# Five-tile openings, a multiply moved to VectorE, ordered store waits and an earlier cast in a linear-attention plus swish-MLP kernel

## The chip, the cores and the metric

The kernel runs on one core of a Trainium2 chip. The metric is device time in microseconds (us) of one execution. All times below are us unless marked ns. The engines are TensorE (PE, with its weight load PEld), VectorE (DVE), ScalarE (ACT), GpSimd (POOL) and SyncE (SP), whose queue issues most DMAs.

## The reference

Eight batches of eight heads, 576 tokens, head size 64. The attention is linear: the softmax of q runs over the head size and the softmax of k over the tokens, so that a 64x64 matrix per head stands between k, v and q. Its output, 4608 tokens of 512 features, goes through a two-layer MLP of width 2048 with the activation h * sigmoid(beta * h), whose beta is one number per hidden feature.

```python
q_s = softmax(q, axis=-1); k_s = softmax(k, axis=2)
kv  = einsum('bhsd,bhse->bhde', k_s, v)
x   = einsum('bhsd,bhde->bhse', q_s, kv)      # -> [4608, 512]
h   = x @ w_in                                # [4608, 2048]
out = (h / (1 + exp(-beta * h))) @ w_out      # [4608, 512]
```

## The kernel before, in words

**Slabs.** The MLP runs over nine slabs of 512 tokens: slab t (0 to 7) holds the first 512 tokens of batch t, and slab 8 the last 64 tokens of all eight batches. While slab t goes through the MLP, the attention of batch t+1 is worked in between, so that its output XT (bf16, features by tokens) is ready when slab t+1 begins.

**Pass 1 of a slab** makes 16 tiles of hidden features. A tile is four matmuls (m = 0 to 3, one for each 128 input features, each reading XT of that m) of 512 columns into one PSUM bank. ACT reads the bank with Silu (L746) into GT, then DVE scales by 1/beta (scale_g, L769) and, on the way, adds pieces of GT up for pass 2 (L800, L805). Tiles rotate over three banks (HB = 0, 1, 2). A slab opens with pass1_lead: the first three tiles side by side, m = 0 of all three, then m = 1, and so on, so that late XT parts are wanted late. The tile after that goes into bank 3, the following ones round the three again.

**Pass 2 of a slab** (pass2_fast, slabs 1 to 8) multiplies GT with w_out as a 2x2 block product in Winograd's form: seven block products of 256-column matmuls (L846) into the bank s and the two banks OB = 3 and 4 (called z5 and z2), and sums and differences of blocks by DVE. g_diff(0) and g_diff(1) (L812, 128x2048, bf16) are two such differences, made in place in GT, and the last two products read them. ACT copies (L882) and DVE adds (L894) move the banks to O2S, which is stored at the slab's end. The last two steps are an ACT copy of z2 and, after the last product, a DVE add of z2.

**The attention in between.** exp of q and k on ACT (L319); a sum of 64 elements (L357), a reciprocal (L359) and a multiply (L361) make the softmax of q. From batch 2 on the multiply runs on POOL, for two head pairs at a time (128x1024), and then SP issues a DMA transpose from EQ to QT (turn, L606). POOL also casts v to bf16 (L377, and L391 for remainders). kv products (L482 for batches 2 and up, two groups of two head pairs), a reciprocal RC (L490) and KVD (L459) on DVE; then the quad: four products of 64x64 tiles (L554) of KVD with QT into two banks, one for each XT part, whose copies go to XT (L596, even parts on DVE, odd ones on ACT). quad(b, (0,)) makes XT parts 0 and 1 from the first two head pairs, quad(b, (1,)) parts 2 and 3 from the others.

**What sets the order.** The program is a list of operations in the order of the Python code; each engine runs its own in that order, and waits on semaphores are derived from reads and writes of named buffers and banks. A list todo of (tick, step) pairs sets the attention steps: tick counts matmuls of the slab from its first (pass 2 by 32/56 for each matmul), and the step is put at that place in all engines' queues. Besides, pass2_fast has numbered hooks 0 to 7 between its products. For batches 2 and 3 (made in slabs 1 and 2) the order is: hook 0 exps; hook 2 sums, multiply and transpose of head pairs 0 and 1; hook 3 the same for 2 and 3 and g_diff(0), then the loads of batch t+3 (SP's queue); at tick 97 or 100 the kv products and g_diff(1); tick 118 the first quad; and after the opening's first matmuls, at tick 1.5 of the next slab, the second quad. In hook 4 ACT loads the Silu table (L1054); in slab 2 batch 4's exps of q come ahead of it.

**Batch 1** is made at the end of slab 0 with the simpler products (L406 for kv, KVD by L449), pair by pair: cast of v on DVE (L377), kv products, RC, KVD, output product.

**The end.** SP waits for all store semaphores (L151) in the order of their names, and then the program ends.

The opening, as it stands:

```python
LEAD = tuple((n, m) for m in range(NM) for n in range(3))

def pass1_lead(t, fs, tick):
    bks = [HB[(hrot[0] + n) % 3] for n in range(3)]
    hrot[0] += 3
    for n, m in LEAD:
        pass1_mm(t, fs[n], m, bks[n])
        tick()
```

Of the kernel before, what the change touches and what calls it, by code (L numbers as in the profile page):

```python
# [18 lines left out]
NF = DFF // 128  # L19
NM = DM // 128  # L20
NG = NF // 2
# [23 lines left out]
class Program:  # L45
# [83 lines left out]
    def emit(self, nc, es):  # L129
        counts, waits = self.plan()  # L130
        sems = {}
        for key in counts:
            sems[key] = es.enter_context(nc.semaphore("s_" + "_".join(str(x) for x in key)))
        by = {e: [] for e in (PE, ACTE, DVE, POOL, SP)}
        for op, w in zip(self.ops, waits):
            by[op.eng].append((op, w))

        def run(eng):
            def body(h):
                for op, w in by[eng]:  # L140
                    for key, n in w:
                        h.wait_ge(sems[key], n)
                    ins = op.fn(h)
                    if op.slot is not None:
                        ins.then_inc(sems[op.count[0]], 16)
                    elif op.inc:
                        ins.then_inc(sems[op.count[0]], 1)
                if eng == SP:
                    for key, n in sorted(counts.items(), key=str):
                        if key[0] == "dma" and str(key[1]).startswith("out"):  # L150
                            h.wait_ge(sems[key], n)  # L151
            return body

        with nc.Block() as blk:
            for e in (PE, ACTE, DVE, POOL, SP):
                getattr(blk, e)(run(e))


def bass_efficient_attn_shen__then__act_swish_beta_kernel(
# [12 lines left out]
    with ExitStack() as es:  # L172
# [48 lines left out]
        HB = (0, 1, 2)  # L221
        OB = (3, 4)
        MB = (5, 6, 7)

        P = Program()
# [376 lines left out]
        def turn(b, hp0, n):  # L602
            i = b % 2
            o = bass.AP(QT[i], hp0 * 512, [[2048, 128], [128, 4 * n], [1, 128]])
            a = bass.AP(EQ[i], hp0 * 512, [[2048, 128], [1, 512 * n]])
            add(SP, lambda e: e.dma_start_transpose(o, a),  # L606
                r=[("eq", i, hp) for hp in range(hp0, hp0 + n)],
                w=[("qt", i, hp) for hp in range(hp0, hp0 + n)], slot=f"tq{i}{hp0}")
# [6 lines left out]
        def norm_turn(b, hp0):  # L615
            norm_main(b, hp0, 2, POOL)
            turn(b, hp0, 2)

        def norm_turn_rem():
            norm_rem()  # L620
            turn_rem()

        def one(fn, *a):
            return lambda: fn(*a)

        def steps(fn, *a):
            return lambda: go(fn(*a))
# [8 lines left out]
        def attn_late(b):  # L636
            if b < 4:
                x = 100 if b == 2 else 97
                return [(x, steps(kv_all, b)), (x + .1, lambda: g_diff(1)),
                        (118, one(quad, b, (0,)))]  # L640
            return [(96, steps(kv_all, b)), (99, lambda: g_diff(1)), (112, one(quad, b))]

# [95 lines left out]
        hrot = [0]  # L738
# [16 lines left out]
                pass1_mm(t, f, m, bk)  # L755
                tick()

        LEAD = tuple((n, m) for m in range(NM) for n in range(3))

        def pass1_lead(t, fs, tick):  # L760
            bks = [HB[(hrot[0] + n) % 3] for n in range(3)]
            hrot[0] += 3
            for n, m in LEAD:
                pass1_mm(t, fs[n], m, bks[n])
                tick()

# [43 lines left out]
        def g_diff(fh):  # L810
            f, th = NG * fh, 1 - fh
            add(DVE, lambda e: e.tensor_tensor(gv(f, th, NG), gv(f, th, NG), gv(f, 1 - th, NG),  # L812
                                               ALU.subtract),
                r=gk(f, 0, NG) + gk(f, 1, NG), w=gk(f, th, NG), war=True)
# [140 lines left out]
        for t in range(NSLAB):  # L955
            todo = []
            if t == 0:
                todo = [(x, steps(t_steps, 1, (hp,), NOW, ACTE))
                        for hp, x in enumerate((97, 106, 114, 119))]
                todo += [(107, one(exp_kr_s, 1))]  # L960
                todo += [(x, one(exp_k, 1, hp, 1)) for hp, x in enumerate((108, 115, 120, 125.5))]
                todo += [(x, one(cast_v, 1, hp, DVE))
                         for hp, x in ((1, 118.5), (2, 123), (3, 127))]
                todo += [(x, steps(kv_steps, 1, (hp,), NOW))
                         for hp, x in enumerate((118, 122, 126))]
                todo += [(x, steps(out_step, 1, hp, NOW, ACTE)) for hp, x in enumerate((122.5, 125))]
                todo += [(117, one(o2_evac, 0, 0, 3, ACTE))]
                todo += [(2, steps(out_step, 0, 3, HEAD, DVE))]
            elif t < 4:
                todo = attn_late(t + 1)  # L970
                if t > 1:
                    todo += [(1.5, one(quad, t, (1,)))]
                if t == 3:
                    todo += [(4, one(norm_turn, 4, 2))]
                if t == 1:
                    todo += [(1, steps(out_step, 1, 2, (3,), ACTE)),
                             (3, steps(kv_steps, 1, (3,), (7,))),
                             (6, steps(out_step, 1, 3, (7,), DVE)),
                             (6.1, one(w_sum, 2, 4, 4)), (6.2, one(w_diff, 0)),
                             (6.3, one(w_diff, 1))]  # L980
            elif t < 7:
                todo = attn(t + 1)
            elif t == 7:
                todo = spread(outr_steps(1), 32, 48)
            todo = sorted(todo, key=lambda x: -x[0])
# [7 lines left out]
            def ftile(n):  # L993
                return n if t == 0 else n // 2 + NG * (n % 2)

            for n in range(NF + 1):
                if n == 0:
                    pass1_lead(t, [ftile(x) for x in range(3)], tick)
                elif 2 < n < NF:
                    pass1_tile(t, ftile(n), tick, 3 if n == 3 else None)  # L1000
                if n:
                    scale_g(ftile(n - 1))
                    for i_, w_ in {8: ((0, 4),), 12: ((4, 2),), 14: ((6, 1),), 16: ((7, 1),)}.get(
                            n if t else 0, ()):
                        g_sum1(i_, w_)
                        g_sum2(i_, w_)
                    if t == 2 and n == 2:
                        for hp in range(NHP):
                            cast_v(3, hp, after=P.writer[("gt", 0, 0)])
                if t == 0 and n == 14:  # L1010
                    w_sum(1)
                if t == 1 and n in (4, 7, 10):
                    o2_evac(0, n // 3, 3 + n // 3, ACTE)
                    if n == 10:
                        store(0)
# [28 lines left out]
            def on(n, fn, *a):  # L1044
                hooks.setdefault(n, []).append(lambda: fn(*a))
# [8 lines left out]
                add(ACTE, lambda e: e.activation(DUMMY[:, 2:3], WARM[:, 0:1], ACT.Silu),  # L1054
                    r=["warm"], w=["dummy"])

            def casts(b):
                g = P.writer[("gs2", NG - 1)]
                if b % 2 == 0:
                    cast_vr(b, after=g)  # L1060
                for hp in range(NHP):
                    cast_v(b, hp, after=g)

            if t == 1:
                on(0, exps, 2)
                on(0, casts, 2)
                on(2, norm_turn, 2, 0)
                on(3, norm_turn, 2, 2)
                on(3, g_diff, 0)
                on(4, silu_table)  # L1070
                on(3, load, 4)
            elif t == 2:
                on(0, exps, 3)
                on(2, norm_turn, 3, 0)
                on(3, norm_turn, 3, 2)
                on(3, g_diff, 0)
                on(3, load, 5)
                on(4, exp_q, 4)
                on(4, silu_table)
                on(4, casts, 4)  # L1080
                on(6, norm_turn, 4, 0)
            elif t == 3:
                on(0, exp_k, 4)
                on(0, exp_kr, 4)
                on(0, exp_q, 5)
                on(3, g_diff, 0)
                on(4, norm_turn, 5, 0)
                on(5, norm_turn, 5, 2)
                on(4, exp_qr, 1)
                on(5, exp_k, 5)  # L1090
                on(5, norm_turn_rem)
                on(5, casts, 5)
                on(5, load, 6)
                on(7, load_rem, "qrf", qt_h, QRF, 4)
            elif t + 2 < B:
                b = t + 2
                on(0, exps, b)
                on(0, casts, b)
                if t == 4:
                    on(0, load, 7)  # L1100
                on(3, norm_turn, b, 0)
                on(4, norm_turn, b, 2)
# [40 lines left out]
```

The softmax here doesn't subtract the row's maximum and nothing guards it: scores larger than these inputs give would overflow.

## Time and profile before

| what | value |
|---|---|
| median of 8 runs | 272.8 us (272.5 to 274.31) |
| the profiled execution's own time | 272.85 us |
| its span, first to last instruction | 271.1 us |
| granted TensorE clock, mean | 0.998 |
| TensorE / VectorE / ScalarE / GpSimd busy | 97% / 71% / 67% / 23% |
| slab 1, pass 2 | about 61 to 75 us |
| slab 2, pass 1 and pass 2 | about 75 to 89 and 89 to 104 us |
| slab 3, pass 1 and pass 2 | about 104 to 118 and 118 to 132 us |

The profile is of one execution. Its span is 1.75 us shorter than that execution's time. "Busy" of TensorE counts the tail of each matmul, which overlaps the next, so that idle time is understated: two matmuls of 512 columns that follow each other at once start 0.216 apart and are shown as 0.379 long. A few matmul records are missing from the trace, among them the first of the openings. In lines of the timeline the columns are start, length, engine, line of the kernel, operation, output and input with their shapes, and the count of merged instructions; in brackets stands the idle time of the engine before it and what ended it.

### The profile page before, as it was taken

Reading aid. Unit: us, or ns where it says so; the run is one execution under the profiler, and the core shown is the slowest. Engines: PE = TensorE matmul, PEld = TensorE weight load, DVE = VectorE, ACT = ScalarE, POOL = GpSimd, SP = SyncE. Lnnn points to the kernel's source line nnn. Section 1 sums busy time; section 2 is a strip of 40 time slices with the busy share of each in tenths; the row PEclk is TensorE's granted clock in tenths of the full one; section 3 lists DMA queues with packets and bytes.
Section 4 is the critical chain, followed back from the end, with each engine's and each line's share of the span. In section 5 each row is a group of like instructions: output and inputs, shape, how many; then the busy total and the mean of one; then the engine's idle time right before and its main releaser. Section 6 shows DMA issues by size and latency. Waiting matters only on the chain.

```text
span 271.1 us, 4991 instructions
## 1 busy us (share of the span) xinstructions
PE 262.1 (97%) x1974; PEld 163.1 (60%) x1993; DVE 193.1 (71%) x407; ACT 181.3 (67%) x289; POOL 63.1 (23%) x80
## 2 busy tenths in 40 slices
PE   8899999999999999999999999999999999999994
PEld 3444444448744875468645864587458745874683
DVE  5964586887967798868778876887588448626762
ACT  4988558789467974887778937892883387018610
POOL 2890010006530089100810660036000100000000
PEclk9999999999999999999999999999999999999999
DMA  7999999999599129940489899503600130012006
GB/s 214 322 205 207 225 327 352 294 257 376 139 325 303 67 49 295 282 155 2 78 278 282 263 357 155 184 4 77 213 2 0 37 139 2 0 59 98 0 1 156
DMA packets 59368, 45.95 MB, mean 170 GB/s; under 512 B 28609, under 2 KB 58321, under 8 KB 58321
## 3 DMA queue, kind: packets, MB, share of 16 engines
q1 hardware_dynamic: 54480, 40.90, 53.3%
q0 software_dynamic: 4240, 4.19, 9.3%
q10 hardware_dynamic: 624, 0.53, 0.6%
q8 instruction: 16, 0.26, 0.4%
q14 instruction: 8, 0.06, 0.1%
HBM read 36.71 MB, written 9.44 MB: 170 GB/s over the span
## 4 chain that ended last, share of the span: by engine, by line
PE 84%; DVE 7%; DMA 2%; ACT 2%; SPq 2%; issue 1%; DVEq 0%
PE PS L406 49%; PE PS L846 33%; DMA VF<-in_v_dram 2%; DVE QS L357 2%; PE PS L482 1%; PE PS L554 1%; DVE GT L812 1%; SPq L290 1%; SPq L278 1%; ACT EQ L319 1%; DVE EQ L361 1%; DVE VB L377 1%; DVE QI L359 0%; ACT L1054 0%; ACT O2S L882 0%
## 5 line engine op out<-in xcount | busy, mean ns | idle before, releaser
L406 PE MATMUL PS<-XT,WIN 128*128 128x512 bf16 x560 | 125.3, 379 | 1.2 <-issue 0.3
L746 ACT ACTIVATE GT<-PS,BETA 128x512 bf16<-128x512 f32 x144 | 95.2, 690 | 39.5 <-PE PS L406 39.2
L406 PEld LDWEIGHTS PS<-XT,WIN 128*128 128x128 bf16 x576 | 54.9, 98 | 64.9 <-DVE XT L596 0.7
L769 DVE TENSOR_SCALAR GT<-GT,RB 128x512 bf16<-128x512 bf16 x144 | 52.8, 387 | 38.3 <-ACT GT L746 37.6
L361 POOL TENSOR_TENSOR EQ<-EQ,QI 128x1024 bf16<-128x1024 bf16 (+1 forms) x13 | 25.6, 1967 | 48.5 <-DVE QI L359 47.8
L846 PE MATMUL PS<-WSUM,GT 128*128 128x256 bf16 x256 | 30.1, 273 | 1.2 <-ACT O2S L882 1.0
L846 PE MATMUL PS<-WOUT,GS 128*128 128x256 bf16 x256 | 31.1, 273 | 0.0
L846 PE MATMUL PS<-WOUT,GT 128*128 128x256 bf16 x256 | 29.8, 273 | 0.0
L846 PEld LDWEIGHTS PS<-WSUM,GT 128*128 128x128 bf16 x256 | 24.8, 98 | 5.2 <-issue 1.3
L882 ACT COPY O2S<-PS 128x512 f32<-128x512 f32 (+1 forms) x17 | 9.4, 559 | 26.1 <-PE PS L846 26.1
L846 PEld LDWEIGHTS PS<-WOUT,GT 128*128 128x128 bf16 x256 | 24.8, 98 | 3.0
L846 PEld LDWEIGHTS PS<-WOUT,GS 128*128 128x128 bf16 x256 | 24.8, 98 | 3.0
L319 ACT ACTIVATE EQ<-QF 128x512 bf16<-128x512 f32 x32 | 17.9, 619 | 7.8 <-DMA QF<-in_q_dram 7.7
L805 DVE TENSOR_TENSOR GS<-GT 128x512 bf16<-128x512 bf16 (+2 forms) x32 | 21.9, 685 | 0.0
L812 DVE TENSOR_TENSOR GT<-GT 128x2048 bf16<-128x2048 bf16 x16 | 21.7, 1383 | 0.0
L377 POOL CAST VB<-VF 128x512 bf16<-128x512 f32 x24 | 15.6, 649 | 21.9 <-DVE GS L805 13.3
L357 DVE TENSOR_REDUCE QS<-EQ 128x16 f32<-128x1024 bf16 (+1 forms) x20 | 19.8, 988 | 0.9 <-ACT EQ L319 0.9
L319 ACT ACTIVATE EK<-KF 128x512 bf16<-128x512 f32 x32 | 18.1, 620 | 0.2
L894 DVE TENSOR_TENSOR O2S<-TS,PS 128x512 f32<-128x512 f32 (+1 forms) x17 | 10.8, 647 | 9.7 <-PE PS L846 9.7
L846 PE MATMUL PS<-WSUM,GS 128*128 128x256 bf16 x128 | 16.6, 273 | 0.0
L406 PE MATMUL PS<-WOUT,GT 128*128 128x512 bf16 x62 | 15.0, 379 | 0.1
L846 PEld LDWEIGHTS PS<-WSUM,GS 128*128 128x128 bf16 x128 | 12.5, 98 | 3.2
(90 smaller groups left out, 207.1 us busy)
## 6 DMA issues: line engine op xcount, KB each, us to landing
out_dram<-O2S SPq DMA_DIRECT2D x8, 1024.0 KB, 4.9
QF<-in_q_dram SPq DMA_DIRECT2D x6, 1024.0 KB, 6.5
KF<-in_k_dram SPq DMA_DIRECT2D x6, 1024.0 KB, 9.3
VF<-in_v_dram SPq DMA_DIRECT2D x6, 1024.0 KB, 12.4
KF<-in_k_dram SPq DMA_DIRECT2D x8, 256.0 KB, 5.6
VF<-in_v_dram SPq DMA_DIRECT2D x8, 256.0 KB, 5.6
WOUT<-in_moe_w_out_dram POOLq DMA_DIRECT2D x4, 512.0 KB, 16.7
WIN<-in_moe_w_in_dram POOLq DMA_DIRECT2D x3, 512.0 KB, 9.4
```

The lines of the kernel that those rows point to most:

```text
L319: add(ACTE, lambda e, o=o, a=a: e.activation(o, a, ACT.Exp), r=[(name + "f", i, hp)], w=[("e" + name, i, hp)])
L357: add(DVE, lambda e: e.tensor_reduce(s_, a, AX.X, ALU.add), r=ks, w=[("qs", i, hp0)])
L361: add(eng, lambda e: e.tensor_tensor(a, a, vb, ALU.mult), r=ks + [("qi", i, hp0)], w=ks)
L377: add(eng, lambda e: (e.copy if eng == ACTE else e.tensor_copy)(o, a), r=[("vf", i, hp), ("vone", i)], w=[("vb", i, hp)], after=after)
L406: add(PE, lambda e: e.matmul(o, l, r_, start=start, stop=stop), r=r, w=w, bank=[bk])
L746: add(ACTE, lambda e: e.activation(GT[:, f, :], PS[bk][:, :], ACT.Silu, scale=BETA[:, f:f + 1]), r=[("ps", bk), "beta"], w=[("gt", f, 0), ...
L769: add(DVE, lambda e: e.tensor_scalar(GT[:, f, :], GT[:, f, :], RB[:, f:f + 1], None, ALU.mult), r=k + ["rb"], w=k)
L805: add(DVE, lambda e: e.tensor_tensor(GS2[:, i:i + n, :], GT[:, i:i + n, :], GT[:, i + NG:i + NG + n, :], ALU.add), r=[k_ for f in (i, i + ...
L812: add(DVE, lambda e: e.tensor_tensor(gv(f, th, NG), gv(f, th, NG), gv(f, 1 - th, NG), ALU.subtract), r=gk(f, 0, NG) + gk(f, 1, NG), w=gk(f ...
L846: add(PE, lambda e, l=l, r_=r_, st=st, u=u, i=i, b_=b_: e.matmul(PS[b_][:, 256 * u:256 * u + 256], l, r_, start=st, stop=end and i == NG - ...
L882: add(eng, lambda e, b_=b_, u0=u0, u1=u1: (e.copy if eng == ACTE else e.tensor_copy)(o[:, u0:u1, :], bank3(b_)[:, u0:u1, :]), r=[("ps", b_ ...
L894: add(DVE, lambda e, b_=b_, u0=u0, u1=u1: e.tensor_tensor(o[:, u0:u1, :], ts[:, u0:u1, :], bank3(b_)[:, u0:u1, :], ALU.add), r=["ts", ("ps ...
```

## The change

Six edits:

1. In slabs 2 and 3 the opening holds five tiles instead of three. The fourth and fifth go into the banks of OB, which pass 2 of the slab before has just left. Its order is m = 0 and m = 1 of four tiles, then both for the fifth, then m = 2 of all five and m = 3 of all five. The second quad moves from tick 1.5 to tick 6, so from behind the second matmul to behind the sixth.
2. For batches 2 and 3 the multiply of head pairs 2 and 3 goes from POOL to DVE and stands behind g_diff(1); the transpose follows it. The sums stay where they were.
3. In slab 1 the loads of batch 4 move from hook 3 to hook 4 and in slab 2 those of batch 5 likewise. In SP's queue they stand behind the transpose, as before.
4. In slab 2 the Silu table load moves from hook 4 to hook 6, behind ACT's copy of z2 and the copy of XT part 1; the casts of batch 4 on POOL wait for the DVE multiply instead of the last GS sum.
5. The cast of batch 1's second value pair goes ahead of RC and KVD of its first pair on DVE (tick 118.5 to 117.9, before the kv step at 118).
6. SP's final waits are ordered by the place of the last store on each semaphore instead of by name.

In slab 3 batch 4's second norm_turn keeps its tick 4, so that its sums now stand ahead of the DVE copy of the second quad, not behind it.

```diff
+        last = {op.count[0]: op.pos for op in self.ops if op.slot is not None}
...
-                    for key, n in sorted(counts.items(), key=str):
-                        if key[0] == "dma" and str(key[1]).startswith("out"):
-                            h.wait_ge(sems[key], n)
+                    for key in sorted((k for k in counts if str(k[1]).startswith("out")),
+                                      key=lambda k: last[k]):
+                        h.wait_ge(sems[key], counts[key])
...
+        def diff_norm(b):
+            g_diff(1)
+            norm_main(b, 2, 2, sums=False)
+            turn(b, 2, 2)
...
-                return [(x, steps(kv_all, b)), (x + .1, lambda: g_diff(1)),
+                return [(x, steps(kv_all, b)), (x + .1, one(diff_norm, b)),
...
-        LEAD = tuple((n, m) for m in range(NM) for n in range(3))
+        LEAD = {3: tuple((n, m) for m in range(NM) for n in range(3)),
+                5: tuple([(n, m) for m in range(2) for n in range(4)] + [(4, 0), (4, 1)]
+                         + [(n, m) for m in range(2, NM) for n in range(5)])}
...
-            bks = [HB[(hrot[0] + n) % 3] for n in range(3)]
+            bks = [HB[(hrot[0] + n) % 3] for n in range(3)] + list(OB)
...
-                         for hp, x in ((1, 118.5), (2, 123), (3, 127))]
+                         for hp, x in ((1, 117.9), (2, 123), (3, 127))]
...
-                    todo += [(1.5, one(quad, t, (1,)))]
+                    todo += [(6, one(quad, t, (1,)))]
...
+            lead = 5 if t in (2, 3) else 3
...
-                    pass1_lead(t, [ftile(x) for x in range(3)], tick)
-                elif 2 < n < NF:
+                    pass1_lead(t, [ftile(x) for x in range(lead)], tick)
+                elif lead <= n < NF:
...
+            def norm_sums(b, hp0):
+                norm_main(b, hp0, 2, mult=False)
+
-            def casts(b):
-                g = P.writer[("gs2", NG - 1)]
+            def casts(b, key=("gs2", NG - 1)):
+                g = P.writer[key]
...
             if t == 1:
-                on(3, norm_turn, 2, 2)
+                on(3, norm_sums, 2, 2)
-                on(3, load, 4)
+                on(4, load, 4)
             elif t == 2:
-                on(3, norm_turn, 3, 2)
+                on(3, norm_sums, 3, 2)
-                on(3, load, 5)
-                on(4, silu_table)
-                on(4, casts, 4)
+                on(4, casts, 4, ("eq", 1, 2))
+                on(4, load, 5)
+                on(6, silu_table)
```

More of the change, by code (lines that the diff above doesn't have):

```diff
@@ L756, in pass1_tile @@
                 tick()
-        LEAD = tuple((n, m) for m in range(NM) for n in range(3))
+        LEAD = {3: tuple((n, m) for m in range(NM) for n in range(3)),
+                5: tuple([(n, m) for m in range(2) for n in range(4)] + [(4, 0), (4, 1)]
+                         + [(n, m) for m in range(2, NM) for n in range(5)])}
         def pass1_lead(t, fs, tick):
-            bks = [HB[(hrot[0] + n) % 3] for n in range(3)]
+            bks = [HB[(hrot[0] + n) % 3] for n in range(3)] + list(OB)
             hrot[0] += 3
-            for n, m in LEAD:
+            for n, m in LEAD[len(fs)]:
                 pass1_mm(t, fs[n], m, bks[n])
```

## The prediction, made before the changed kernel ran

> **What bounds the kernel now.** I read the summary of the page first, then the chain of work that ended last, then the waits, and then, for the four places that the diff touches, the timelines of TensorE (PE), VectorE (DVE), ScalarE (ACT), GpSimd (POOL) and SyncE's DMA queue (SP).
>
> ```profile
> PE 262.1 (97%) x1974; PEld 163.1 (60%) x1993; DVE 193.1 (71%) x407; ACT 181.3 (67%) x289; POOL 63.1 (23%) x80
> PE 84%; DVE 7%; DMA 2%; ACT 2%; SPq 2%; issue 1%; DVEq 0%
> ```
>
> TensorE is busy for 97% of the span at full granted clock and makes 84% of the chain. The number of matmuls doesn't change, so the change can win only what TensorE now waits, and loses whatever new waits it puts there. TensorE's timeline shows three waits near the edited lines (start, length, then in brackets the idle time before and its releaser):
>
> ```profile
> 43.32 0.39 PE L406 MATMUL PS<-VB,EK 128*128 128x131 bf16 x4 [0.34 <-DVE VB L377]
> 73.09 1.91 PE L846 MATMUL PS<-WSUM,GT 128*128 128x256 bf16 x16 [0.23 <-DVE GT L812]
> 102.09 1.92 PE L846 MATMUL PS<-WSUM,GT 128*128 128x256 bf16 x16 [0.99 <-ACT O2S L882]
> ```
>
> The idle time is a little less than the loss, because a matmul's tail counts as busy. I count from starts: matmuls of one product start 0.11 apart (256 columns) or 0.216 (512 columns). The matmul before 73.09 starts at 72.58, so 0.51 - 0.11 = 0.40 is lost; the one before 102.09 starts at 100.82, so 1.27 - 0.11 = 1.16 is lost.
>
> **Batch 1's second value (cast L377).** At 42.29 DVE runs RC (L490) and KVD (L449), and then the cast of value pair 1 at 42.76 (0.42 long); TensorE resumes 0.14 after its end. Put ahead, the cast starts at 42.29, where the WSUM add lets DVE go (41.69 + 0.60), ends at 42.71, and TensorE resumes at 42.85: **-0.47**. TensorE's own queue is ready then (three matmuls from 42.16 end their turn at 42.81). The value must have landed: its load is issued at 36.70 and such loads take 5.6 (median), so 42.3, just in time. Behind the cast RC and KVD come 0.35 later; KVD ends at 43.19, and its reader, the output product that started at 43.82, now wants it at 43.35. The later casts keep their place in the DVE queue and their loads are there by then.
>
> **First opening (end of slab 1, start of slab 2).** DVE's second difference (L812) and POOL's second multiply (L361), beside a difference of slab 3 with POOL idle and DVE's own multiply of half the size:
>
> ```profile
> 69.10 2.76 POOL L361 TENSOR_TENSOR EQ<-EQ,QI 128x1024 bf16<-128x1024 bf16 x1
> 70.82 2.12 DVE L812 TENSOR_TENSOR GT<-GT 128x2048 bf16<-128x2048 bf16 x1
> 126.28 1.22 DVE L812 TENSOR_TENSOR GT<-GT 128x2048 bf16<-128x2048 bf16 x1
> L361 DVE TENSOR_TENSOR EQ<-EQ,QI 128x512 bf16<-128x512 bf16 x4 | 2.8, 691 | 0.1
> ```
>
> The difference takes 2.12 instead of 1.22 while POOL multiplies (until 71.86) and ends 1.08 after it: it stood until POOL was through. Without that multiply it ends at 70.82 + 1.22 = 72.04, before TensorE wants it at 72.69: **-0.40**.
>
> In its place DVE multiplies 128x1024. No row shows that. Above it is POOL's 1.90 (undisturbed, at 95.41), below it DVE's bf16 add of 128x1024 (L824, 0.69). The same line at half the size takes 0.69; DVE's reduce grows from 0.67 to 1.20 between these sizes. I take 0.69 + 0.53 = **1.22**, an estimate from the nearest row. It starts at 71.97 (DVE operations of this length start 1.15 apart) and ends at 73.19; before, POOL was through at 71.86. The transpose behind it is issued 0.03 later and lands 3.2 after its issue:
>
> ```profile
> QT<-EQ SPq DMA_TRANSPOSE x2, 3.2
> ```
>
> So QT lands at 76.42. The old quad started at 75.36, after two matmuls (of which one record is missing); the new one stands after six, and without a wait would start at 75.36 - 0.40 + 4 x 0.216 = 75.82. It waits 0.60. The seventh matmul of the opening starts 0.34 after the quad, at 76.76; before, it started at 75.70 + 4 x 0.216 = 76.56. Up to here the opening is **0.20 later**: the wait that went comes back as a wait for the transpose. The copies of the quad (ACT, DVE, some 1.2 from its start) are done by the eleventh matmul, which first needs them. Batch 4's loads stand behind this transpose in SP's queue and start 1.3 later; their reader, the exp at 97.9, has over 10 us to spare.
>
> **Five tiles at once.** With three tiles, tile 0 gets its last matmul as the tenth, at 77.21, and ACT starts on it 0.44 later:
>
> ```profile
> 77.65 3.71 ACT L746 ACTIVATE GT<-PS,BETA 128x512 bf16<-128x512 f32 x6 [1.17 <-PE PS L406]
> ```
>
> In a row, activations start 0.57 apart and take 0.69; TensorE makes a tile in 0.86. With five tiles, tile 0 is done only at matmul 16 and five tiles within 0.86. Count from there: bank 0 is free at 0.44 + 0.69 + 0.05 = 1.18, and matmul 21 wants it at 1.08: wait 0.10. Tile 5, in the same bank, is sixth on ACT: start 3.31, end 4.00; matmul 33, which wants its bank, is ready at 3.77 and goes at 4.05: wait 0.28. Together **+0.38**, in each of the two openings. With three tiles bank 0 is wanted 7 x 0.216 = 1.51 after the tenth matmul, and nothing waits. Bounds: 0 and, if each of the eleven later tiles waited 0.10, 1.1; I keep 0.38.
>
> **Second opening (end of slab 2, start of slab 3).** The table load (1.28, at 100.06) now stands behind the copy that TensorE waited for; the copy follows the exps, ends at 100.62, and TensorE wants it at 100.93: **-1.16**. The difference there also had 2.12 and ends at 100.33 instead. But DVE has no gap here, so its next steps follow at the distances of the timeline: multiply at 100.26, XT copy 101.41, output add 102.01, sum 102.61, reciprocal 103.85, output add 104.02, then, new, batch 4's second sum 104.63 and reciprocal 105.87 ahead of the quad's XT copy, since that sum keeps its place after four matmuls while the quad moves from the second to the sixth. The copy starts at 106.04 and ends at 106.73. The transpose (multiply end 101.48, landing 104.71) holds the quad, ready at 104.37 - 1.16 + 0.86 = 104.07, for 0.64. The eleventh matmul, ready at 105.91, waits for the copy until 106.78. Before, it started at 104.71 + 8 x 0.216 = 106.44: **+0.34** net. The casts of batch 4 on POOL now wait for the multiply, 1.2 later; their products come after 124.
>
> A page of the Trainium skill, "GPSIMD Engine Reference", section 4.1 (Engine selection), says that GpSimd takes about twice VectorE's time for an elementwise operation with two inputs. By it the multiply would be 1.90 / 2 = 0.95 (an estimate by that page), 0.27 less in each opening, and the sum 0.54 smaller; the 0.69 of the half-size row speaks against that.
>
> Another page, "SBUF — State Buffer", section "Who interferes with whom", speaks against putting the multiply on VectorE: with two SBUF inputs it would stand for the whole of a GpSimd instruction that reads SBUF. The DVE multiply at 8.76 took 0.92 beside a POOL multiply, against 0.69. At both new places POOL has nothing to run, since the casts are held back.
>
> **The ordered store waits.** SP's six waits at the end: one of 1.80 from 268.55, then four short ones, the last at 270.58. With the last store's wait put last these four fall before the landing: 270.58 - 270.35 = **-0.23** (bounds -0.23 and 0).
>
> **Sum.** -0.47 + (0.20 + 0.38) + (0.34 + 0.38) - 0.23 = +0.60. The profiled execution took 272.85 (span 271.1), which is 0.05 above the median of 272.8: **273.5** after.
>
> **Rivals.** Within 0.3% (0.82 us), about what a measurement here can tell from nothing, is called "same".
> - *No backlog* (14%): ACT's late banks hold nobody: 273.45 - 0.76 = 272.7, same. For: ACT is busy only 67%. Against: the 0.57 spacing.
> - *The waits are covered* (15%): the multiply at 0.69 brings each opening 0.53 and there is no backlog: 273.45 - 1.06 - 0.76 = 271.6; if no new wait is left at all, 272.85 - 0.47 - 0.40 - 1.16 - 0.23 = 270.6. Against: 3.2 of transpose after a multiply that can't start before the difference.
> - *DVE pays POOL's price* (13%): the multiply takes 1.90; each opening pays 0.68 more at the quad or the copy: 274.8, slower. From 1.33 on it leaves "same". If the difference keeps its 2.12 because something other than POOL made it wait, so that the change doesn't do what it says, the cost is similar, 0.9 in each.
> - *The value lands late* (7%): if it lands after 42.76, the first gain is gone, and RC and KVD behind the cast are late too: 273.9, slower.
>
> The forecast has 51%; its own spread, 273.0 to 274.0, lies for 35 of these within 0.3% and for 16 above. So faster 0.15, same 0.35 + 0.14 = 0.49, slower 0.16 + 0.13 + 0.07 = 0.36. The range 272.2 to 274.3 leaves out most of the covered case and the dear multiply.
>
> **What will show it.** The difference at 1.22 and behind it a DVE multiply of about 1.22 in both slabs; TensorE's first matmul of slab 2 starting early and its quad waiting for the transpose; in slab 3 a wait for DVE's XT copy ahead of matmul 11; a wait for an activation twelve matmuls after the opening. I am wrong if the quad starts without a wait, if that copy runs ahead of the sum, or if the activations keep up.

## The result and the profile after

The changed kernel takes 274.23 us (median of 12 runs, 273.19 to 275.02), the kernel before 272.78 (33 runs). The ratio is 1.0046, with a 95% interval of 1.0033 to 1.0060: slower by some 1.25 us by the ratio; the two medians lie 1.45 apart. A second measurement beside other kernels gave 1.0060 (1.0048 to 1.0072). The profiled execution took 273.91, its span is 272.1.

TensorE's work and clock are as before. In the summary and in the shares of the chain of waits, VectorE's share of the chain has grown from 7% to 11%, TensorE's has shrunk from 84% to 82%:

```profile
PE 263.2 (97%) x1974; PEld 163.4 (60%) x1993; DVE 192.1 (71%) x409; ACT 180.7 (66%) x289; POOL 56.5 (21%) x78
PE 82%; DVE 11%; ACT 3%; DMA 1%; issue 1%; DVEq 0%
```

VectorE is busy for less time in all, and more of that time is on the path. TensorE's timeline of the changed kernel no longer shows the three waits that the prediction listed, and has four others (start, length, engine, line, operation; in brackets idle time before and its releaser):

```profile
72.08 0.41 PE L555 MATMUL PS<-QT,KVD 64*64 64x512 bf16 x4 [0.46 <-DMA QT<-EQ]
76.50 0.41 PE L555 MATMUL PS<-QT,KVD 64*64 64x512 bf16 x4 [0.75 <-DMA QT<-EQ]
105.40 0.41 PE L555 MATMUL PS<-QT,KVD 64*64 64x512 bf16 x4 [0.57 <-DMA QT<-EQ]
107.31 7.04 PE L407 MATMUL PS<-XT,WIN 128*128 128x512 bf16 x30 [0.53 <-DVE XT L597]
```

Three quads wait for a transpose and one opening for a copy. VectorE around the first opening, and around the second:

```profile
70.24 1.22 DVE L820 TENSOR_TENSOR GT<-GT 128x2048 bf16<-128x2048 bf16 x1
71.37 1.22 DVE L362 TENSOR_TENSOR EQ<-EQ,QI 128x1024 bf16<-128x1024 bf16 x1
```

```profile
105.21 1.21 DVE L358 TENSOR_REDUCE QS<-EQ 128x16 f32<-128x1024 bf16 x1
106.45 0.25 DVE L360 RECIPROCAL QI<-QS 128x16 f32<-128x16 f32 x1
106.62 0.63 DVE L597 CAST XT<-PS 128x512 bf16<-128x512 f32 x1
```

The difference is down from 2.12 to 1.22, and the multiply behind it takes 1.22, to the digit what the half-size row gave. In the second fence the sum and the reciprocal stand ahead of the copy that TensorE waits for.

The weight loads of slab 2's opening show the activations' backlog (engine PEld, same columns):

```profile
76.50 0.11 PEld L555 LDWEIGHTS PS<-QT,KVD 64*64 64x64 bf16 x4 [1.25 <-DMA QT<-EQ]
...
79.97 2.27 PEld L407 LDWEIGHTS PS<-XT,WIN 128*128 128x128 bf16 x12 [0.41 <-ACT GT L752]
82.86 0.11 PEld L407 LDWEIGHTS PS<-XT,WIN 128*128 128x128 bf16 x2 [0.62 <-ACT GT L752]
```

Two waits for an activation, twelve matmuls apart, as the count gave. From the starts of the matmuls they cost 0.08 and 0.29.

**The ledger.** The same matmul is looked up in both profiles, and the difference of its start (after minus before) is followed along the kernel. The last column is the change of that difference, the middle one what the prediction had for it.

| up to | after minus before | predicted step | seen step |
|---|---|---|---|
| pass 2 of slab 1 | 60.39 - 60.97 = -0.58 | -0.47 | -0.58 |
| first quad of slab 1 | 72.08 - 72.23 = -0.15 | none | +0.43 |
| opening of slab 2 | 74.51 - 75.05 = -0.54 | -0.40 | -0.39 |
| seventh matmul | 76.84 - 76.56 = +0.28 | +0.60 | +0.82 |
| pass 2 of slab 2 | 89.94 - 89.27 = +0.67 | +0.38 | +0.39 |
| opening of slab 3 | 103.58 - 104.06 = -0.48 | -1.16 | -1.15 |
| eleventh matmul | 107.31 - 106.44 = +0.87 | +1.50 | +1.35 |
| pass 2 of slab 3 | 119.53 - 118.28 = +1.25 | +0.38 | +0.38 |
| last add of DVE | 268.74 - 267.50 = +1.24 | 0 | -0.01 |
| end of the span | 272.11 - 271.05 = +1.06 | -0.23 | -0.18 |
| sum | | +0.60 | +1.06 |

From slab 3 on nothing happens until the end. The step that was not foreseen is the second row: slab 1's first quad, on which TensorE gives most of the early cast back.

The first row is not the cast alone. From batch 1's first cast to its second it is 2.02 before and 1.55 after, which is the predicted -0.47; another 0.12 is there because the first value landed earlier in this profile (first cast at 40.62 against 40.74). Such shifts come without an edit: in two runs below whose code is the kernel before's up to this place (*the store waits alone*, *the table load alone*) pass 2 of slab 1 is at 60.51 and 60.52, against 60.97. So what counts in the ledger is the single step; the +1.06 is the difference of two executions.

### The profile page after: what moved, and what is told of

Its sections match the earlier page's. It is cut to its first block, busy times and chain, and to the rows that moved or that the text cites. A ratio compares the mean times of both kernels' runs of the same rounds, so it can differ in the third digit from the quotient of the medians.

```text
span 272.1 us, 4989 instructions
## 1 busy us (share of the span) xinstructions
PE 263.2 (97%) x1974; PEld 163.4 (60%) x1993; DVE 192.1 (71%) x409; ACT 180.7 (66%) x289; POOL 56.5 (21%) x78
## 4 chain that ended last, share of the span: by engine, by line
PE 82%; DVE 11%; ACT 3%; DMA 1%; issue 1%; DVEq 0%
PE PS L407 50%; PE PS L854 29%; DVE QS L358 3%; ACT GT L752 3%; DVE GT L820 2%; DMA QT<-EQ 1%; DVE EQ L362 1%; PE PS L555 1%; PE PS L483 1%; DVE QI L360 1%; PE PS L405 1%; DVE O2S L902 1%; DVE TS L923 1%; DVE TS L926 1%; DVE XT L597 0%
## 5 line engine op out<-in xcount | busy, mean ns | idle before, releaser
L777 DVE TENSOR_SCALAR GT<-GT,RB 128x512 bf16<-128x512 bf16 x144 | 51.8, 380 | 39.7 <-ACT GT L752 38.9
L362 POOL TENSOR_TENSOR EQ<-EQ,QI 128x1024 bf16<-128x1024 bf16 (+1 forms) x11 | 20.0, 1823 | 47.8 <-DVE QI L360 47.3
L820 DVE TENSOR_TENSOR GT<-GT 128x2048 bf16<-128x2048 bf16 x16 | 19.9, 1268 | 0.0
```

Source lines behind the costliest of these rows:

```text
L362: add(eng, lambda e: e.tensor_tensor(a, a, vb, ALU.mult), r=ks + [("qi", i, hp0)], w=ks)
L777: add(DVE, lambda e: e.tensor_scalar(GT[:, f, :], GT[:, f, :], RB[:, f:f + 1], None, ALU.mult), r=k + ["rb"], w=k)
```

## The experiments

Ten runs. Theory A is the prediction's account, in which everything up to batch 4 keeps its distance from TensorE; theory B adds that in slab 1 the transposes stand behind loads still in flight, so that time won before them is lost at the quad. Ratios are to the kernel before, run on the same chip, in five rounds each. The changed kernel's own ratio came out as 1.0046 and 1.0060 in two measurements, so that small differences between ratios settle little, and the profiles decide.

**The cast alone** (kernel before):

```diff
-                         for hp, x in ((1, 118.5), (2, 123), (3, 127))]
+                         for hp, x in ((1, 117.9), (2, 123), (3, 127))]
```

> The kernel before with one edit: batch 1's second value cast ahead of its first pair's RC and KVD. My forecast prices it at -0.47 us. Theory A (TensorE's chain): everything up to batch 4 is timed from TensorE, so the gain holds to the end: ratio about 0.9983, and the first quad of slab 1 starts without a wait. Theory B (loads in flight): the first transpose of slab 1 lands at a time that batch 3's loads set, so that the gain of the cast is eaten at the first quad (a wait of some 0.4 us there): ratio 0.9995 to 1.0005.

Measured: 0.9988 (0.9970 to 1.0005), which does not tell the theories apart. The profile does. The cast's wait is gone, and at the first quad of slab 1 stands

```profile
72.25 0.41 PE L554 MATMUL PS<-QT,KVD 64*64 64x512 bf16 x4 [0.72 <-DMA QT<-EQ]
```

at 72.25, where it stood at 72.23 before. The gain of the cast is eaten there, as B says. The old wait of 0.40 for the second difference, a product later, is now hidden behind the quad's wait: one wait may cover another. Slab 3's quad stands 0.37 earlier than in the kernel before (104.00 against 104.37), but in *the store waits alone*, whose code is unedited up to there, it stands 0.46 earlier (103.91), so that this gain is not shown to be the cast's. B holds for the wait, and its ratio of about 1 lies within the interval.

**The store waits alone** (kernel before, the first hunk of the change's diff):

> The kernel before with one edit: the final store waits in the order of the last stores. Forecast -0.23 us, ratio 0.9992; in the profile the time from the last DVE add to the final branch falls from 2.73 to about 2.5 us. The rival says that the last landing sets the end anyway and the short waits fall after it in any order: no change in that distance.

Measured: 0.9986 (0.9974 to 0.9999). SP's final waits in the kernel before and here (shortest/median/longest in ns, first and last start):

```profile
L151 SPq EVENT_SEMAPHORE  x6: 17/28/1800, 268.5 to 270.6; - x6
L152 SPq EVENT_SEMAPHORE  x6: 17/28/28, 268.6 to 270.0; - x6
```

From the end of the last DVE add to the final branch it is 2.59, against 2.73 in the kernel before. Over all profiles this distance is 2.73 to 2.82 with the waits in the order of names (three) and 2.49 to 2.61 in the new order (nine): 0.23 on average. From the last store's landing to that branch it is 0.31 or 0.32 in the three and 0.08 or 0.09 in the nine. The rival falls.

**The sum behind the copy** (changed kernel):

```diff
-                    todo += [(4, one(norm_turn, 4, 2))]
+                    todo += [(6.5, one(norm_turn, 4, 2))]
```

> The changed kernel with one edit: in slab 3 batch 4's second sum, reciprocal, multiply and transpose at tick 6.5 instead of 4, so that DVE copies the second quad's XT part ahead of that sum. My account puts 0.70 us on this order (TensorE's start-to-start gap of 0.91 ahead of matmul 11 instead of 0.22): ratio to the kernel before about 1.0020, where the changed kernel has 1.0046, and that gap gone. The rival says that the quad, which waits for its transpose, is what holds the opening, and that the copy is late in any order: gain under 0.2 us.

Measured: 1.0025 (1.0009 to 1.0041), 0.0021 below the changed kernel's ratio. VectorE now waits for the quad, and TensorE's matmuls behind the quad run on without a break:

```profile
107.02 0.69 DVE L597 CAST XT<-PS 128x512 bf16<-128x512 f32 x1 [0.53 <-PE PS L555]
```

```profile
106.55 0.41 PE L555 MATMUL PS<-QT,KVD 64*64 64x512 bf16 x4 [0.55 <-DMA QT<-EQ]
106.89 1.48 PE L407 MATMUL PS<-XT,WIN 128*128 128x512 bf16 x6
```

The 0.70 ahead of matmul 11 came from the order on VectorE alone. In this run the two transposes of slab 1 landed later still (4.55 and 4.88 after issue), so that its span of 272.6 is no shorter than the changed kernel's.

**Five banks** (changed kernel):

```diff
-                    pass1_tile(t, ftile(n), tick, 3 if n == 3 else None)
+                    pass1_tile(t, ftile(n), tick, 3 if n == 3 else
+                               OB[n - 8] if lead == 5 and n in (8, 9) else None)
```

> The changed kernel with one edit: in slabs 2 and 3 tiles 8 and 9 go into the two banks of OB, so that no tile needs a bank of the opening's queue of activations except tiles 5 to 7. My account: the wait of 0.29 us at matmul 33 of each of the two slabs goes and that of 0.08 at matmul 21 stays: -0.58 us, ratio to the kernel before about 1.0025. The rival says that ScalarE's backlog only moves the wait to a later tile (its 16 activations must all be done by the slab's end): gain under 0.15 us.

Measured: 1.0016 (1.0002 to 1.0029), 0.0030 lower (0.0021 expected). Weight loads that waited for an activation between 78 and 86, in the changed kernel and then here (total, times, longest):

```profile
PEld PS L407 <- ACT GT L752: 1.0, 2, 0.6
```

```profile
PEld PS L407 <- ACT GT L752: 0.4, 1, 0.4
```

One of the two waits is gone and does not come back at a later tile: a tile takes TensorE 0.86 and the activations start 0.57 apart, so that ScalarE catches up. The rival falls.

**v later** (changed kernel): batch 3's load of v behind slab 1's transposes.

```diff
-                load(3)
+                load_main("qf", qt_h, QF, 3)
+                load_main("kf", kt_h, KF, 3)
...
+                on(4, load_main, "vf", vt_h, VF, 3)
                 on(4, load, 4)
```

> The changed kernel with one edit: batch 3's load of v (1 MB) is issued in slab 1 behind both transposes, ahead of batch 4's loads, instead of at the end of slab 0. Theory B (in slab 1 the first transpose stands behind batch 3's loads and the first store in the DMA queues): the store lands some 3 us earlier, the first transpose lands 3.1 to 3.2 after its issue instead of 3.6 to 4.5, and TensorE's gap ahead of the first quad of slab 1 falls from 0.74 (1.70 in another run) to 0.25 to 0.31; ratio to the kernel before 1.0046 - 0.0016 = 1.0030 or lower. The rival, that a transpose is slow there for another reason (its own rate, TensorE's reads beside it): the gap stays over 0.6 and the ratio at 1.0046.

Measured: 1.0039 (1.0024 to 1.0054), which alone settles nothing. The quads of slab 1:

```profile
71.92 0.41 PE L555 MATMUL PS<-QT,KVD 64*64 64x512 bf16 x4
...
76.16 0.41 PE L555 MATMUL PS<-QT,KVD 64*64 64x512 bf16 x4 [0.57 <-DMA QT<-EQ]
```

The first no longer waits (start to start 0.30, 0.74 in the changed kernel). Its transpose, issued at 68.73, landed 3.15 later; the first store had landed at 68.74 instead of 71.13. The row of that transpose (number, us to landing), in the changed kernel and then here:

```profile
QT<-EQ SPq DMA_TRANSPOSE x1, 3.6
```

```profile
QT<-EQ SPq DMA_TRANSPOSE x1, 3.1
```

B holds for the first quad. The second still waits, since that one is made late by VectorE's chain.

**The multiply back on POOL** (changed kernel, edit 2 and the casts' new wait undone):

```diff
             g_diff(1)
-            norm_main(b, 2, 2, sums=False)
-            turn(b, 2, 2)
...
-                on(3, norm_sums, 2, 2)
+                on(3, norm_turn, 2, 2)
...
-                on(3, norm_sums, 3, 2)
+                on(3, norm_turn, 3, 2)
...
-                on(4, casts, 4, ("eq", 1, 2))
+                on(4, casts, 4)
```

> The changed kernel with one part undone: batches 2 and 3 have their second multiply on POOL in hook 3 again, with the transpose behind it; five-tile openings, table load, cast and store waits stay. My account: the second difference is 2.12 long again (1.22 in the changed kernel) and TensorE waits for it, 0.1 to 0.4 in slab 1 and 0.3 in slab 2, but the second transposes are issued 1.2 us earlier and neither second quad waits (0.82 and 0.64 in the changed kernel): ratio to the kernel before about 1.0020. The rival, that VectorE is the better place for it as such: slower than the changed kernel, over 1.0060.

Measured: 1.0006 (0.9993 to 1.0018), 0.0040 or 1.1 us below the changed kernel: more than expected. TensorE's timeline around the two openings:

```profile
72.17 0.41 PE L555 MATMUL PS<-QT,KVD 64*64 64x512 bf16 x4 [0.51 <-DMA QT<-EQ]
72.51 2.03 PE L852 MATMUL PS<-WSUM,GT 128*128 128x256 bf16 x17
74.59 1.24 PE L407 MATMUL PS<-XT,WIN 128*128 128x512 bf16 x5
75.76 0.41 PE L555 MATMUL PS<-QT,KVD 64*64 64x512 bf16 x4
```

```profile
101.31 1.91 PE L852 MATMUL PS<-WSUM,GT 128*128 128x256 bf16 x16 [0.26 <-DVE GT L818]
103.27 1.24 PE L407 MATMUL PS<-XT,WIN 128*128 128x512 bf16 x5
104.45 0.41 PE L555 MATMUL PS<-QT,KVD 64*64 64x512 bf16 x4
104.79 1.04 PE L407 MATMUL PS<-XT,WIN 128*128 128x512 bf16 x4
106.34 1.04 PE L407 MATMUL PS<-XT,WIN 128*128 128x512 bf16 x4 [0.51 <-DVE XT L597]
```

Neither second quad waits. The differences are 2.12 again, but in slab 1 nobody waits for that one, because the first quad's wait covers it (the product runs on from 72.51), and in slab 2 it costs 0.43 (0.54 from start to start). So VectorE was the worse place for this multiply, not as an engine but because there it stands behind the difference, and the transpose behind it.

**The table load alone** (kernel before):

```diff
-                on(4, silu_table)
                 on(4, casts, 4)
+                on(6, silu_table)
```

> The kernel before with one edit: in slab 2 the table load goes from hook 4 to hook 6, behind the copies. My account: the wait of 1.16 ahead of slab 2's last product falls to about 0.3, since the difference under POOL's multiply ends only 0.3 after the moment at which TensorE is ready; at the opening of slab 3 VectorE, which has no gap, makes the quad's copy no earlier, so that some 0.3 is lost again: gain 0.4 to 0.8 us, ratio 0.9971 to 0.9985. The rival, that the whole 1.16 goes: ratio 0.9957.

Measured: 0.9980 (0.9969 to 0.9991). The wait ahead of slab 2's last product is down from 1.16 to 0.45 and has another releaser:

```profile
100.92 1.91 PE L846 MATMUL PS<-WSUM,GT 128*128 128x256 bf16 x16 [0.27 <-DVE GT L812]
```

A further 0.18 is lost at the opening of slab 3, where the copy is late. The rival's whole 1.16 does not come.

**The combination** (kernel before, POOL multiplies and three tiles): early cast, ordered waits, table load in hook 6, v later, and in slab 3 batch 4's two sums behind the quad. Of the edit, the parts not shown above:

```diff
-                    todo += [(4, one(norm_turn, 4, 2))]
+                    todo += [(3.9, one(norm_turn, 4, 0)), (4, one(norm_turn, 4, 2))]
...
-                on(4, silu_table)
                 on(4, casts, 4)
-                on(6, norm_turn, 4, 0)
+                on(6, silu_table)
```

> The kernel before (multiply on POOL, three-tile openings) with the parts that I take for gains: early cast, ordered store waits, table load in hook 6, and two edits of mine: batch 3's load of v behind the transposes of slab 1, and batch 4's sums of slab 3 behind the second quad's copy. My account: -0.4 for the cast (now not eaten at the first quad), -0.2 for the waits, -0.9 for the table load: about -1.5 us, ratio 0.9945, faster than both kernels. The rival, that each gain is only shifted to the next wait: ratio over 0.9980.

Measured: 271.49 us, 0.9946 (0.9934 to 0.9958): faster than both kernels by 1.4 and some 2.7 us. What remains near the openings are the two waits for a difference that POOL holds up:

```profile
72.68 1.91 PE L847 MATMUL PS<-WSUM,GT 128*128 128x256 bf16 x16 [0.23 <-DVE GT L813]
```

```profile
100.97 1.91 PE L847 MATMUL PS<-WSUM,GT 128*128 128x256 bf16 x16 [0.28 <-DVE GT L813]
...
103.24 0.41 PE L555 MATMUL PS<-QT,KVD 64*64 64x512 bf16 x4
103.58 4.72 PE L407 MATMUL PS<-XT,WIN 128*128 128x512 bf16 x21
```

They are dear (0.40 and 0.45), but cheaper than the second quads' waits that the change put in their place (0.82 and 0.64).

**The changed kernel mended** (changed kernel with the edits of *five banks*, *the sum behind the copy* and *v later*):

> The changed kernel with three of the edits tried singly: tiles 8 and 9 in the banks of OB, batch 4's second sum behind the quad's copy, batch 3's load of v behind the transposes. If the priced waits add up: 0.58 + 0.70 + 0.45 = 1.7 us less than the changed kernel, ratio to the kernel before about 0.9985, still behind the combination with the multiply on POOL (0.9946), since both second quads keep their waits of 0.6 for a transpose behind the VectorE multiply. The rival, that these waits overlap so that only the largest counts: ratio 1.0020 or more.

Measured: 0.9990 (0.9970 to 1.0009), 0.0056 below the changed kernel's first ratio and 0.0070 below the one measured beside it: the three waits add up, and the rival falls. Of what the change added, the wait of 0.08 in each backlog and both second quads' waits are left:

```profile
76.37 0.41 PE L555 MATMUL PS<-QT,KVD 64*64 64x512 bf16 x4 [0.92 <-DMA QT<-EQ]
```

**The changed kernel again:**

> The changed kernel again, unedited, beside the mended one on the same chip, to see how far its time and the landing of its transposes in slab 1 vary by themselves. By my account the three waits for data that don't depend on the loads (0.64, 0.70 and twice 0.37 in the profile) are the same to 0.05, and only the gaps ahead of the two quads of slab 1 differ from the first profile (0.74 and 1.13): ratio 1.0030 to 1.0060.

Measured: 1.0060 (1.0048 to 1.0072). In its profile the second opening's quad waits 0.63, the copy 0.71, the backlogs 0.37 and 0.37; slab 1's quads have gaps of 0.90 and 1.06 (0.74 and 1.13 in the first profile). The waits that hang on engines repeat; those that hang on the landing in slab 1 move.

## Why the prediction was right and where it was wrong

- **The difference held up by POOL, and the multiply at 1.22.** Right: 1.22 and 1.22 in both slabs, and 2.12 again with the multiply back on POOL. The half-size row was the right base. The rival in which VectorE pays POOL's price, and the one in which the change does nothing to the difference, fall. The Trainium skill's page "GPSIMD Engine Reference", section 4.1 (Engine selection), would have made it 0.95 (1.90 / 2, an estimate by that page): here the ratio of the two engines is 1.90 to 1.22, so 1.56, not two.
- **The second quads wait for the transpose.** Right in kind, and in slab 3 in size (0.64 as predicted). In slab 1 the step "lands 3.2 after its issue" was too short: it took 3.84 in the changed kernel. Of the 0.64 more, 0.43 had been lost at the first quad already, so the wait is 0.82 instead of 0.60. The profile before had a row against a fixed 3.2: the transpose issued at 107.22, behind batch 5's loads, landed 8.1 after its issue.
- **Where the cast's gain goes.** This is the step that was missing. The prediction let the -0.47 run to the end. In fact the first quad of slab 1 had no slack before: it started 0.04 after its transpose landed (72.19, 72.23), as every quad that waits does, and 0.30 after the matmul ahead of it, where slab 3's first quad (128.35), whose transpose had long landed, starts 0.20 after. I had not asked what came next on that path. That alone would not have eaten the gain, since the transpose's issue moves with TensorE: it comes 8.23 or 8.24 after the first matmul of pass 2 in all twelve profiles. What failed is the landing. In the changed kernel the transpose took 3.58 instead of 3.15, and the quad waited those 0.43. The cast alone and the later load of v show it.
- **The backlog of five tiles.** Right: 0.08 + 0.29 against 0.10 + 0.28, in both slabs, and the larger one goes with two more banks.
- **The table load.** Right: -1.15 seen against -1.16, since the difference no longer lags there; with POOL's multiply kept, only 0.71 of it comes.
- **Sum and copy on VectorE.** Right: the wait is 0.70, and 0.87 was predicted; the output add and the copy took 0.63 each instead of 0.69.
- **The store waits.** Right: 0.23 on average.
- **The whole.** The mechanism of each priced step was right and the sum, +0.60, was too small: two landings in slab 1 took 0.4 to 0.6 longer than the rows of before. So the likeliest case, a change too small to tell, did not come. The measured 274.23 lies above the forecast's own spread (273.0 to 274.0) and 0.07 below the upper end of its range, which it met with some luck, since no rival had a late transpose.

**Open.** Why batch 3's loads end late in slab 1. In every profile with the early cast and v loaded early (six) they ended at 68.6 to 69.8, after the first transpose's issue, and the transpose took 3.55 to 4.55. In the three without the early cast the loads ended at 66.9 to 67.4 and it took 3.14 or 3.15; with v loaded later it took 3.14 or 3.15 in all three. In the six it landed 3.38 or 3.39 after the last of these loads, to the hundredth alike while its time from issue varied by 1.0. So the loads set that landing, and moving one of them confirms it; why they end later with the earlier cast is not shown. It is not that the transpose comes too early: in *the store waits alone* and *the table load alone*, without the early cast, it was issued at 68.59 and 68.58, as early as with it (68.37 to 68.61 in the six), and the loads were through.

The second transpose of slab 1 took 3.11 to 3.17 in the six profiles with the multiply on POOL and 3.23 to 4.88 in the six with it on VectorE; in slab 2 it took 3.14 to 3.18 with the multiply on VectorE. A 16 KB packet of the instruction queue falls near the packets of slab 1's second transpose in all twelve profiles: at their end with the multiply on POOL; with it on VectorE ahead of them in five and at their end in one. In *v later* it came ahead and the transpose took only 3.23. No run varied that packet, and the cause stays open.

## What to carry to other kernels

A wait that is taken off the critical engine is worth only what is left until the next release on that engine: list, for each place after it, by how much its data comes ahead of need, the landings of transposes and loads above all (here the first quad had no slack), and ask whether that landing moves along with the gain or is set by something else (here loads, 3.38 before it). Moving an operation off a slow engine doesn't pay if on the fast one it queues behind the very operation that was to be sped up and a long transfer follows it: here the difference won 0.90 and the transpose was issued 1.28 later (72.62 against 71.34 with the multiply on POOL). When more work is put ahead of a late input, count the banks and the consumer's rate, and look at which operations of other engines keep their old place in the queue.

## What the runs showed of the hardware that was not expected

- One transpose of 128x1024 bf16 between two SBUF tiles mostly lands 3.1 to 3.3 us after its issue. In slab 1 it took 3.55 to 4.55 where batch 3's loads were still in flight at its issue, on the same queue, and landed 3.38 or 3.39 after the last of them. In slab 3, issued while batch 5's loads were in flight, the first one took 8.1 to 10.0 in the twelve profiles.
- A semaphore wait on SP that is already satisfied costs some 0.06 us (the last four of the kernel before start 0.06 apart): ordering the final waits by landing was worth 0.23 us.
- VectorE's wait for POOL is shown as VectorE's own busy time: the difference has 2.12 instead of 1.22 on the page, so that the stall appears in no list of waits of that engine.
